# An FFT mixing and balanced mixture-of-experts kernel: pieces of the last fold and of the weight turns, lists of eight in the rounds, and another pace for the gathers

## The chip, the cores and the metric

The kernel runs on one core of a Trainium2 chip. Its time is the device time of one execution in microseconds (us). The kernel before took 535.88 us, the median of three runs (535.51 to 536.1). All five engines of the core take part: TensorE (PE in the profile), VectorE (DVE), ScalarE (ACT), GpSimd (POOL) and SyncE (SP). Each engine works through its own list of instructions in order and waits for the others by semaphores. "PEclk" in the profile is the share of TensorE's full clock that was granted.

## The reference

The input x has 8 batches of 2496 rows by 256 columns. The first step takes the real part of a two-dimensional Fourier transform of each batch; its 19968 rows are the tokens of the second step.

```python
X = np.fft.fft(x, axis=1); X = np.fft.fft(X, axis=2); x = X.real
logits = x @ w_gate                       # 19968 tokens, 8 experts
order = np.argsort(-logits.flatten())     # best pair of token and expert first
for idx in order:
    tok, e = idx // E, idx % E
    if assigned[tok] >= 0 or counts[e] >= cap: continue    # cap = 2496
    assigned[tok] = e; counts[e] += 1
for e in range(E):
    out[assigned == e] = np.maximum(x[assigned == e] @ w1[e], 0) @ w2[e]
```

Every expert takes exactly 2496 tokens: an expert that is full turns tokens away, and they fall to their next choice. The hidden width is 1024.

## The kernel before

**Front (0 to about 90 us).** For each batch `b`, SP and POOL load the rows and their mirror image (`a_t`, `b_t`), and DVE adds them (the fold, L343 and L344). Folded, a batch is 10 blocks of 128 rows, in 5 groups of 2 (index `i` in the change). `zb` is then summed from the fold (L361, L362). `turn_x` transposes the folded batch on PE in three chunks (tp, L285) and ACT copies them out (zt, L287). `gate_x` multiplies the three chunks by the gate's table (yps, L295), into three column groups of one output tile, and ACT copies the result (yt, L298 and L299). `place_y` transposes and stores it as a high and a low part (ytp L305, yhl L308 and L309). In the loop, `gate_x` of batch b - 1 stands between the second and the third chunk of batch b. Behind the loop follow the logits (lps, L452 to L455) and their copy `lg` (L469), laid out as 128 partitions by 8 experts by 160 columns.

**Middle (about 100 to 172 us).** `unit()` issues one of 40 transform units: PE products (fftps, L1038), sums and differences on DVE (stage, L1021 and L1022), and copies on ACT and POOL. It alternates with `first_chain()`, which makes the first choice of experts on DVE: `choose` (each token's best expert), `count` (how many tokens exceed the cap), `lowest` (the lowest logits in each partition, transposed into `lt` on PE, L627), `search` (each turn tries 16 thresholds for each expert and counts, L646, then combines on PE, L657), and `first_strips`, which fixes the tokens that are certain (lev_ps L839, rps L854). The functions are generators. Each `yield` gives an estimated DVE cost, and `yield SYNC` marks the places where PE must wait for DVE. `unit()` keeps two clocks from these estimates and decides how many units come ahead of each step. Four of the units also issue `turn_w`, which folds the transform's last table into an expert's first weight (wps, L1058, four times two matmuls, evicted on ACT). `sort_call` (sps, L1098) gathers the tokens that are certain into strips, which serve as tiles of 384 rows of one expert.

**Experts (172 us to the end).** `experts()` walks over 40 strip tiles of 384 rows and 16 late tiles. Tile j is treated in three parts; in each, `up` does part of the first product of tile j (hps, L1234) and `down` one block of 128 rows of the second product of tile j - 1 (ops, L1257). The result goes to an output tile of a ring, and POOL writes its rows by an indirect DMA, the scatter (L1261). A full tile has three scatters. `take` evicts each product on ACT or DVE, whichever has less estimated work (L995 on ACT, L999 and L1001 on DVE).

Beside the strip tiles run the three rounds of `settle_rest()`, which settle the uncertain tokens: `choose`, `lowest`, `search`, `settle` (the new threshold, transposed on PE at L690), then the token lists of the late tiles (`slots`, `inverse` with inv_ps at L766). `pace(j)` issues these steps by credit: each part of a tile adds 1.9 (at most 3.0), each step takes its estimate off, and a `SYNC` ends the part. When the steps are through, at tile `placed[0]`, the ring grows from 8 output tiles to 18, and `feed` may issue the late tiles' gathers, three indirect DMAs on POOL for each (L1210). They go onto POOL's list between the scatters, and `turn` transposes what they bring (L1222) shortly before the late tile is used. The condition that paces gather m is

```python
j >= min(max(placed[0] + 1 + m * (51 - placed[0]) // 15, 0 if m < 8 else 32), 38 + m)
```

Of the kernel before, what the change touches and what calls it, by code (L numbers as in the profile page):

```python
# [8 lines left out]
FT = mybir.dt.float32  # L9
BF = mybir.dt.bfloat16  # L10
# [25 lines left out]
K_PEN = 1.0e20  # L36
# [17 lines left out]
KC = 56  # L54
# [14 lines left out]
def kernel(  # L69
# [220 lines left out]
    def gate_x(b, zts):  # L290
        yps = psl.tile([P, 4, P], FT, tag="y", bufs=2, name="yps")
        for blk in range(2):
            for c, zt in enumerate(zts):
                nn = 4 if c < 2 else 2
                nc.tensor.matmul(yps[32 * c:32 * c + 32, 0:nn, :], lhsT=g_sb[:, blk, :], rhs=zt[:, blk, 0:nn, :],  # L295
                                 start=(blk == 0), stop=(blk == 1))
# [44 lines left out]
    for b in range(B):  # L341
        a_t, b_t = ab.pop(b)
        nc.vector.tensor_tensor(a_t[:, :, :, 1:D], a_t[:, :, :, 1:D], b_t[:, :, ::-1, D - 1:0:-1], op=AL.add)  # L343
        nc.vector.tensor_tensor(a_t[:, :, :, 0], a_t[:, :, :, 0], b_t[:, :, ::-1, 0], op=AL.add)  # L344
# [17 lines left out]
        nc.vector.tensor_tensor(zb[:, :, P + 1:D], pv[:, :, 1:P], pv[:, :, D - 1:P:-1], op=AL.subtract)  # L362
        zts[b] = [turn_x(b, pv, 0), turn_x(b, pv, 1)]
        if b > 0:
            gate_x(b - 1, zts.pop(b - 1))
# [154 lines left out]
    off = dd.rearrange("p e c -> p (e c)").bitcast(BF)[:, 0:E * GC].rearrange("p (e c) -> p e c", c=GC)  # L520
    ohb = asg.tile([P, E, GC], BF, name="ohb")
    mx = asg.tile([P, GC], FT, name="mx")
    tree = asg.tile([P, 4, GC], FT, name="tree")
    lists = asg.tile([P, E, 8], FT, name="lists")
    lists_x = asg.tile([P, 8, P], FT, name="lists_x")
    cjunk = asg.tile([P, P], BF, name="cjunk")
# [52 lines left out]
    def choose(first):  # L579
        if first:  # L580
            src = lg
        else:
            nc.vector.tensor_tensor(off, lg, tsel[:, :, None].to_broadcast([P, E, GC]), op=AL.is_lt)
            yield 1.5
            nc.vector.scalar_tensor_tensor(wa, in0=off, scalar=-K_PEN, in1=lg, op0=AL.mult, op1=AL.add)
            yield 1.5
            src = wa
# [5 lines left out]
        yield 1.2  # L593
        nc.vector.tensor_tensor(off, src, mx[:, None, :].to_broadcast([P, E, GC]), op=AL.is_lt)
        yield 1.5
        chosen["src"] = src

    def count():
        cps = misc()
        for c in range(0, GC, NG):  # L600
            nc.tensor.matmul(cps[:, 0:P], lhsT=onesb, rhs=off[:, :, c:c + NG], start=(c == 0), stop=(c + NG == GC))
        less = small("less")
        nc.vector.scalar_tensor_tensor(cjunk, in0=cps[:, 0:P], scalar=-1.0, in1=bdiag, op0=AL.mult, op1=AL.mult,
                                       accum_out=less)
        nc.vector.tensor_scalar(exc, in0=less, scalar1=float(P * GC - CAP), scalar2=None, op0=AL.add)
# [3 lines left out]
    def lowest(deep_):  # L609
        nc.vector.scalar_tensor_tensor(wa, in0=off, scalar=-K_LOW, in1=chosen["src"], op0=AL.mult, op1=AL.subtract)  # L610
        yield 1.5
        step = 32 // deep_
        for e in range(E):
            nc.vector.max(lists[:, e, :], wa[:, e, :])
            if e % 4 == 3:
                yield 1.3
            if (e + 1) % step == 0:
                es = slice(e + 1 - step, e + 1)
                nc.vector.tensor_copy(lists_x.rearrange("p j (e g) -> p j e g", g=NG)[:, 0:deep_, es, :],
                                      lists[:, es, 0:deep_].rearrange("p e j -> p j e")[:, :, :, None].to_broadcast(  # L620
                                          [P, deep_, step, NG]))
                yield 0.5
        yield SYNC
        count()
        lt = psr[0].tile([P, deep_, P], FT, tag="lt", bufs=1, name="lt")
        for j in range(deep_):
# [6 lines left out]
        nc.vector.tensor_reduce(lo0, lt[:, deep_ - 1, :], axis=AXX, op=AL.max)  # L633
        wid = small("wid")
        nc.vector.tensor_tensor(wid, hi0, lo0, op=AL.subtract)
        yield 1.2
        found["low"], found["wid"], found["lo0"], found["n"] = lo0, wid, lo0, deep_ * P

    def search(turns):
        junk = wa.rearrange("p e c -> p (e c)")[:, 0:found["n"]]  # L640
        for _ in range(turns):
# [12 lines left out]
            yield 0.9 + found["n"] / 850.0  # L654
# [8 lines left out]
    def settle():  # L663
        low, wid, lo0, ltf = found["low"], found["wid"], found["lo0"], found["ltf"]
        junk = wa.rearrange("p e c -> p (e c)")[:, 0:found["n"]]
# [4 lines left out]
        yield 0.4 + found["n"] / 850.0  # L670
        nc.vector.scalar_tensor_tensor(junk, in0=junk, scalar=-1.0e34, in1=ltf, op0=AL.mult, op1=AL.add)
        yield 0.1 + found["n"] / 900.0
        best = small("best", 8)
        nc.vector.max(best, junk)
        yield 0.1 + found["n"] / 900.0
# [11 lines left out]
        yield 1.6  # L687
# [3 lines left out]
        nc.vector.tensor_scalar(tsel, in0=bps[:, 0:P:NG], scalar1=-1.0, scalar2=None, op0=AL.mult)  # L691
        yield 0.2

    def round_steps(deep_, turns):
        yield from choose(False)
        yield from lowest(deep_)
        yield from search(turns)
# [41 lines left out]
    def inverse(hi1, lo1, pay, w, ncol):  # L739
        ramp8 = ramps[8]  # L740
        inv_ps = psr[0].tile([P, 512], FT, tag="lt", bufs=1, name="inv_ps")
        for c0 in range(0, ncol, 8):
# [6 lines left out]
            o_eq = moe.tile([P, 8, EW + 2], BF, tag="pt", bufs=2, name="o_eq")  # L749
            if w <= P:  # L750
                o_hi = o_eq.rearrange("p a b -> p (a b)")[:, 0:8 * w].rearrange("p (h c) -> p h c", c=8)
                nc.vector.tensor_tensor(o_hi, ramp8[:, 0:w, :], hi1[:, None, cs].to_broadcast([P, w, 8]),
                                        op=AL.is_equal)
                nc.vector.tensor_tensor(o_hi, o_hi, pay[:, None, cs].to_broadcast([P, w, 8]), op=AL.mult)
                o_hi = o_hi.rearrange("p h c -> p c h")
            else:
                o_hi = o_eq[:, :, 0:w]
# [646 lines left out]
```

## Time and profile before

| | us |
|---|---|
| median of three runs | 535.88 |
| the profiled execution | 536.1 |
| its span, first to last instruction | 534.3 |
| PE busy in the span | 471.8 (88%) |
| DVE busy | 372.7 (70%) |
| ACT busy | 337.9 (63%) |
| POOL busy | 313.9 (59%) |

The profile is one execution, taken by the hardware profiler. Its span is 1.8 us shorter than the time of that execution; the rest lies outside the first and last instruction. A line of a group view names the source line, engine, operation, tiles and shapes, then the count, the busy time and the mean duration in ns, then the idle time of the engine just before these instructions and what ended it. A line of a timeline gives start and duration in us, and in square brackets the idle time before it. A table by stretch gives, for each stretch of the span, its length and the busy time and number of instructions of each engine, then the granted clock, the share of the DMA engines and GB/s. In a list of waits, the columns are the total time, how many waits, and the longest.

### The profile page before, as it was taken

To read this page: it belongs to the slowest core of one execution; us is meant where nothing else is said; L and a number is where in the kernel's file an instruction comes from. 1 tells how busy PE (TensorE), PEld (TensorE's weight loads), DVE (VectorE), ACT (ScalarE), POOL (GpSimd) and SP (SyncE) were. 2 spreads that over 40 slices of the span, in tenths; PEclk is the share of its full clock that TensorE was granted. 3 is DMA by queue.
4 is the path that set the end of the run, shared out by engine and by line. 5 is a ranking of instruction groups with operands and counts; after the bars stand their busy time and mean duration, and the time that the engine had idled before them with its cause. 6 is when DMAs were issued, how large, how long until landed. Compare 5 with 4: busy or idle time off the path is not lost.

```text
span 534.3 us, 11232 instructions
## 1 busy us (share of the span) xinstructions
PE 471.8 (88%) x4039; PEld 357.7 (67%) x4039; DVE 372.7 (70%) x952; ACT 337.9 (63%) x762; POOL 313.9 (59%) x362
## 2 busy tenths in 40 slices
PE   0567659899789899999899999999999999999983
PEld 0544436776568566777667877777777777777753
DVE  7799994687978969889978757566654555555431
ACT  7879983156368778788767776556555555555531
POOL 7888815253122555555524336777677777777774
PEclk9968898999989999999989999999999999999988
DMA  8999929078578697523322323342222222222221
GB/s 259 317 281 319 310 89 159 2 240 291 140 217 261 161 225 163 137 95 103 99 76 100 99 88 102 113 130 85 82 83 78 79 87 84 79 69 78 77 77 53
DMA packets 35168, 74.62 MB, mean 140 GB/s; under 512 B 6115, under 2 KB 14349, under 8 KB 35104
## 3 DMA queue, kind: packets, MB, share of 16 engines
q0 software_dynamic: 23296, 42.10, 30.2%
q1 hardware_dynamic: 11808, 31.73, 17.7%
q8 instruction: 33, 0.54, 0.4%
q14 instruction: 31, 0.25, 0.2%
HBM read 51.26 MB, written 32.24 MB: 156 GB/s over the span
## 4 chain that ended last, share of the span: by engine, by line
PE 70%; DVE 13%; ACT 9%; issue 4%; DMA 3%; POOL 1%; POOLq 0%; DVEq 0%; ACTq 0%
PE hps L1234 24%; PE ops L1257 24%; PE sps L1098 5%; PE fftps L1038 5%; PE wps L1058 2%; PE tp L285 2%; ACT zt L287 2%; DMA xa<-in_x_dram 2%; PE yps L295 1%; ACT tf L254 1%; POOL out_dram L1261 1%; DVE xa L343 1%; PE inv_ps L766 1%; DVE stage L1022 1%; PE tp L1222 1%
## 5 line engine op out<-in xcount | busy, mean ns | idle before, releaser
L995 ACT ACTIVATE hb<-hps 128x384 bf16<-128x384 f32 (+1 forms) x326 | 146.2, 493 | 50.5 <-PE hps L1234 47.4
L1257 PE MATMUL ops<-w2t,hb 128*128 128x256 bf16 (+1 forms) x1344 | 175.3, 274 | 0.0
L1257 PEld LDWEIGHTS <-hb 128*128 128x128 bf16 (+1 forms) x1344 | 133.3, 100 | 32.6 <-issue 0.5
L1261 POOL DMA_INDIRECT out_dram<-zball,rid x85 | 89.3, 1051 | 82.7 <-ACT zball L995 63.8
L1234 PE MATMUL hps<-xs,zball 128*128 128x384 bf16 x640 | 127.3, 327 | 0.0
L1234 PEld LDWEIGHTS <-zball 128*128 128x128 bf16 x896 | 86.1, 98 | 43.4 <-issue 2.9
L999 DVE TENSOR_SCALAR hb<-hps 128x384 bf16<-128x384 f32 (+1 forms) x122 | 66.3, 549 | 47.2 <-PE hps L1234 39.2
L129 POOL DMA_INDIRECT xb<-in_x_dram,mir_i x40 | 54.3, 1357 | 11.9 <-issue 10.5
L995 ACT ACTIVATE zball<-ops 128x256 f32<-128x256 f32 (+1 forms) x79 | 30.4, 384 | 31.6 <-PE ops L1257 29.0
L1234 PE MATMUL hps<-xt,zball 128*128 128x384 bf16 (+1 forms) x256 | 48.4, 322 | 0.0
L285 PE MATMUL tp<-identf,xa 128*128 128x128 f32 x160 | 27.4, 336 | 20.1 <-issue 9.2
L285 PEld LDWEIGHTS tp<-identf,xa 128*128 128x128 f32 x160 | 23.6, 176 | 27.1 <-issue 10.2
L995 ACT ACTIVATE xs<-sps 128x384 bf16<-128x384 f32 x68 | 30.4, 493 | 16.0 <-PE sps L1098 15.7
L1026 POOL COPY stage<-stage 128x258 bf16<-128x258 bf16 x40 | 17.7, 447 | 36.3 <-DVE stage L1021 33.0
L1098 PE MATMUL sps<-pt,xl 128*128 128x192 bf16 x320 | 33.8, 246 | 0.7 <-DVE pt L1076 0.7
L1076 DVE TENSOR_SCALAR pt<-rampw,spot 128x193 bf16<-128x193 bf16 x160 | 32.5, 298 | 1.6 <-PE inv_ps L766 0.9
L1098 PEld LDWEIGHTS <-xl 128*128 128x128 bf16 x320 | 27.6, 98 | 3.5 <-issue 1.6
L1210 POOL DMA_INDIRECT xg<-t_dram,ids_l x24 | 23.1, 964 | 7.3 <-issue 7.3
L1261 POOL DMA_INDIRECT out_dram<-zball,rows_l x23 | 22.3, 969 | 7.3 <-issue 2.4
L1044 ACT COPY ev<-fftps 128x512 f32<-128x512 f32 x20 | 11.7, 584 | 22.9 <-PE fftps L1038 15.5
L1001 DVE COPY zball<-ops 128x256 f32<-128x256 f32 (+1 forms) x29 | 12.3, 424 | 19.4 <-PE ops L1257 19.4
L1024 ACT ACTIVATE stage<-stage 128x254 bf16<-128x254 bf16 x40 | 15.6, 414 | 13.3 <-DVE stage L1021 11.6
(356 smaller groups left out, 781.1 us busy)
## 6 DMA issues: line engine op xcount, KB each, us to landing
t_dram<-stage SPq DMA_DIRECT2D x20, 512.0 KB
xl<-t_dram SPq DMA_DIRECT2D x20, 512.0 KB
xa<-in_x_dram SPq DMA_DIRECT2D x8, 1024.0 KB
w1raw<-in_moe_w_dram POOLq DMA_DIRECT2D x8, 512.0 KB, 5.3
w2t<-in_moe_w_dram POOLq DMA_DIRECT2D x8, 512.0 KB, 6.3
xa<-in_x_dram SPq DMA_DIRECT2D x8, 224.0 KB
out_dram<-zball,rid POOLq DMA_INDIRECT x85, 2.5
xb<-in_x_dram,mir_i POOLq DMA_INDIRECT x40, 8.0
```

The source lines that it names most:

```text
L129: nc.gpsimd.indirect_dma_start(out=bv[0:n, i, :], out_offset=None, in_=x_pairs, in_offset=bass.IndirectOffsetOnAxis(ap=mir_i[0:n, b * NK + ...
L285: nc.tensor.transpose(tp[:, blk, u, :], pv[:, 4 * c + u, blk * P:(blk + 1) * P], identf)
L995: nc.scalar.activation(dst, src, ACT.Relu if relu else ACT.Copy)
L999: nc.vector.tensor_scalar(dst, in0=src, scalar1=0.0, scalar2=None, op0=AL.max)
L1026: nc.gpsimd.tensor_copy(st[:, :, 1 + q, 0:P + 1], st[:, :, 3 * q, 0:P + 1])
L1038: nc.tensor.matmul(fps[:, :, d0:d1], lhsT=tab[:nv, i, ks], rhs=zball[:nv, b0:b0 + NB, 2 * i + r, d0:d1], start=(i == 0), stop=(i == NK - 1))
L1076: nc.vector.tensor_scalar(marks[n][:, f, 0:EW + 1], in0=rampw[:, 0:EW + 1], scalar1=spot[:, c:c + 1], scalar2=None, op0=AL.is_equal)
L1098: nc.tensor.matmul(sps[:, j2 * EW:(j2 + 1) * EW], lhsT=xl[:, 2 * g + cc, j2 * P:(j2 + 1) * P], rhs=pt[:, 2 * g + cc, 0:EW], start=(cc == 0 ...
L1210: nc.gpsimd.indirect_dma_start(out=xg[0:nr, q, :], out_offset=None, in_=t_dram, in_offset=bass.IndirectOffsetOnAxis(ap=d["ids"](q, nr), ax ...
L1234: nc.tensor.matmul(hps[:, 0:n], lhsT=w1t[d["e"]][:, j2, fc * P:(fc + 1) * P], rhs=d["x"](j2), start=(j2 == 0), stop=(j2 == 1))
L1257: nc.tensor.matmul(ops[0:nr, 0:D], lhsT=d["hid"][:, fc, b0:b0 + nr], rhs=w2t[d["e"]][:, fc, :], start=(fc == 0), stop=(fc == F // P - 1))
L1261: put = nc.gpsimd.indirect_dma_start(out=out, out_offset=bass.IndirectOffsetOnAxis(ap=d["rows"](b0 // P)[0:nr], axis=0), in_=ot[0:nr, :], ...
```

## The change

It has four parts.

- In the front, the last batch's fold (b = 7) is made in three pieces (groups 0 and 1, 2 and 3, 4), and the gate product of batch 6 is moved ahead of the last batch's transposes. `gate_x` goes through the chunks in the outer loop and through the two halves in the inner one.
- In the middle, the weights of experts 0 to 3 are turned in 16 pieces of two matmuls and one eviction, one after each of the units 15 to 22, 26 to 29 and 33 to 36, instead of whole turns after the units 18, 22, 28 and 34.
- In the rounds, the lists hold 8 values per partition and expert throughout (4 before, in the rounds), so the search and settle passes are 1024 wide instead of 512; there are three search turns in a round instead of two, and one more in the first settling. The choice works expert by expert and sums as it goes (`cnt`), and `count` takes one fp32 product of these sums instead of ten bf16 products over the whole table. The late lists have 64 values per partition instead of 56, hence 8 blocks in `inverse` instead of 7, and their one-hot tiles are written in another layout. Several estimates are changed.
- The gathers are paced at one for every 1.5 tiles from the tile behind `placed[0]`.

```diff
-        for blk in range(2):
-            for c, zt in enumerate(zts):
+        for c, zt in enumerate(zts):
+            for blk in range(2):
...
-        nc.vector.tensor_tensor(a_t[:, :, :, 1:D], a_t[:, :, :, 1:D], b_t[:, :, ::-1, D - 1:0:-1], op=AL.add)
-        nc.vector.tensor_tensor(a_t[:, :, :, 0], a_t[:, :, :, 0], b_t[:, :, ::-1, 0], op=AL.add)
+        for i0, i1 in ((0, 2), (2, 4), (4, NK)) if b == B - 1 else ((0, NK),):
+            nc.vector.tensor_tensor(a_t[:, i0:i1, :, 1:D], a_t[:, i0:i1, :, 1:D], b_t[:, i0:i1, ::-1, D - 1:0:-1],
+                                    op=AL.add)
+            nc.vector.tensor_tensor(a_t[:, i0:i1, :, 0], a_t[:, i0:i1, :, 0], b_t[:, i0:i1, ::-1, 0], op=AL.add)
...
+        if b == B - 1:
+            gate_x(b - 1, zts.pop(b - 1))
         zts[b] = [turn_x(b, pv, 0), turn_x(b, pv, 1)]
-        if b > 0:
+        if 0 < b < B - 1:
             gate_x(b - 1, zts.pop(b - 1))
...
-            nc.vector.tensor_tensor(off, lg, tsel[:, :, None].to_broadcast([P, E, GC]), op=AL.is_lt)
-            nc.vector.scalar_tensor_tensor(wa, in0=off, scalar=-K_PEN, in1=lg, op0=AL.mult, op1=AL.add)
+            for e in range(E):
+                nc.vector.tensor_scalar(wa[:, e, :], in0=lg[:, e, :], scalar1=tsel[:, e:e + 1], scalar2=0.0,
+                                        op0=AL.add, op1=AL.min)
+            nc.vector.scalar_tensor_tensor(wa, in0=wa, scalar=K_PEN, in1=lg, op0=AL.mult, op1=AL.add)
...
-        nc.vector.tensor_tensor(off, src, mx[:, None, :].to_broadcast([P, E, GC]), op=AL.is_lt)
+        for e in range(E):
+            nc.vector.scalar_tensor_tensor(dd[:, e, :], in0=src[:, e, :], scalar=0.0, in1=mx, op0=AL.add,
+                                           op1=AL.is_lt, accum_out=cnt[:, e:e + 1])
+        nc.vector.tensor_copy(cnt_x.rearrange("p (e g) -> p e g", g=NG), cnt[:, :, None].to_broadcast([P, E, NG]))
...
-        for c in range(0, GC, NG):
-            nc.tensor.matmul(cps[:, 0:P], lhsT=onesb, rhs=off[:, :, c:c + NG], start=(c == 0), stop=(c + NG == GC))
+        nc.tensor.matmul(cps[:, 0:1], lhsT=cnt_x, rhs=onesf, start=True, stop=True)
...
+    def finish_round():
+        yield from search(1)
+        yield from settle()
+
-    def round_steps(deep_, turns):
+    def round_steps():
         yield from choose(False)
-        yield from lowest(deep_)
-        yield from search(turns)
+        yield from lowest()
+        yield from search(3)
         yield from settle()
...
-        yield from settle()
+        yield from finish_round()
         for _ in range(NROUND - 1):
-            yield from round_steps(4, 2)
+            yield from round_steps()
...
+    TURNS = (*range(15, 23), *range(26, 30), *range(33, 37))
+    pieces = (None for e in range(4) for _ in turn_pieces(e, "A"))
...
-            if clock["n"] in (18, 22, 28, 34):
-                turn_w((18, 22, 28, 34).index(clock["n"]), "A")
-                clock["PE"] += 2.0
+            if clock["n"] in TURNS:
+                next(pieces)
+                clock["PE"] += 0.45
...
-        while m < len(late) and placed and j >= min(max(placed[0] + 1 + m * (51 - placed[0]) // 15, 0 if m < 8 else 32), 38 + m):
+        while m < len(late) and placed and j >= min(max(placed[0] + 1 + (3 * m) // 2, 0 if m < 8 else 32), 38 + m):
```

## The prediction

> **What bounds the kernel now.** I read the page first: TensorE (PE) is busy for 88% of the span and the chain that ended last gives it 70%. That hides a second limit, so next came the table of busy time by stretch, POOL's timeline, PE's waits and DVE's groups by shape.
>
> The stretches (length, then busy time and count for PE, PE's weight loads, DVE, ACT, POOL, then PE's granted clock):
>
> ```profile
> 77.80:80.90 3.10, 0.82 (x9) 0.84 (x9) 3.10 (x4) 1.52 (x5) 0.61 (x1) 1.00 0.00 0
> 80.90:84.30 3.40, 3.40 (x19) 2.28 (x19) 2.10 (x2) 2.03 (x2) 3.40 (x8) 0.50 0.73 107
> 149.10:152.60 3.50, 3.50 (x19) 2.45 (x18) 1.75 (x5) 1.84 (x5) 1.56 (x3) 0.51 0.77 173
> 178.00:181.40 3.40, 1.35 (x12) 1.10 (x13) 2.81 (x10) 1.04 (x3) 2.65 (x3) 1.00 0.01 1
> 268.60:272.00 3.40, 3.40 (x16) 2.09 (x15) 1.62 (x4) 2.46 (x5) 0.00 (x0) 0.50 0.44 147
> 328.10:529.10 201.00, 195.82 (x1642) 151.34 (x1639) 106.27 (x240) 106.78 (x229) 151.11 (x155) 0.99 0.27 88
> ```
>
> In the last row POOL looks 75% busy, but its timeline shows indirect DMAs at a fixed step, about 0.97 us of work and 0.30 us of issue. From the first gather at 328.16 to the end of the last scatter:
>
> ```profile
> 328.16 1.01 POOL L1210 DMA_INDIRECT xg<-t_dram,ids_l  x1 [0.31 <-issue]
> 329.48 0.97 POOL L1210 DMA_INDIRECT xg<-t_dram,ids_l  x1 [0.30 <-issue]
> ...
> 351.18 0.97 POOL L1261 DMA_INDIRECT out_dram<-zball,rid  x1 [0.57 <-DVE zball L1001]
> 352.46 0.98 POOL L1210 DMA_INDIRECT xg<-t_dram,ids_l  x1 [0.30 <-issue]
> ...
> 528.13 0.93 POOL L1261 DMA_INDIRECT out_dram<-zball,rows_l  x1 [0.30 <-issue]
> ```
>
> That is 155 DMAs (48 gathers, 107 scatters) in 200.9 us. Summing the idle stretches beyond 0.30 us gives 2.89 us, so a step costs (200.9 - 2.89) / 155 = 1.2775 us and POOL has been full since 328. PE runs at the same pace because its output tiles and late inputs pass through POOL. The end is therefore the time at which POOL meets the first gather, plus the number of DMAs from there times 1.2775, plus 5.2 us to the end of the span and 1.8 us outside it (the profiled run: 536.1 us, span 534.3).
>
> PE's waits ahead of that, by line (total, times, longest):
>
> ```profile
> PE wps L1058 <- ACT zball L995: 2.6, 2, 2.1
> PE misc L690 <- DVE trun L686: 2.1, 1, 2.1
> PE lev_ps L839 <- DVE s_lev L834: 1.3, 1, 1.3
> PE rps L854 <- DVE ohb L844: 1.0, 1, 1.0
> ...
> PE misc L601 <- DVE dd L594: 2.7, 1, 2.7
> PE tp L1222 <- DMA xs<-t_dram,ids_l: 2.3, 2, 1.4
> ```
>
> The last line is the last gather coming late (0.82 and 1.45 us near 511). The others say where PE lost time before POOL became the limit.
>
> **The gathers: +6.1 us.** The change paces gathers at 1.5 strip tiles each, from the tile after the lists are placed. The longer rounds place them later: in the changed kernel's instruction order the first gather stands behind 73 scatters (three for each of tiles 0 to 23, and one), where it stood behind 61. Behind it stand 48 gathers and 95 scatters, 143 DMAs in place of 155. The slot after the 73rd scatter is, in the trace of before, the one at 352.46. So POOL would end at 352.46 + 143 x 1.2775 = 535.14 instead of 529.06: +6.1 us, less s, the time by which PE reaches that place earlier. The same by parts: 24.3 later, 15.3 less to issue, 2.9 no longer idle. The step is certain to 0.01 us (gathers 0.96 + 0.30, scatters 0.98 + 0.30), 1.4 us over 143.
>
> After the first gather, a strip tile has 3 scatters and two thirds of 3 gathers, 5 x 1.2775 = 6.39 us of POOL against 5.44 us of PE (two tiles took 10.87). Up to tile 47, POOL falls 22 x 0.95 = 21 us behind, then regains 1.6 us a tile. The last gather has 30 scatters behind it (before: 14), so it is issued at about 535 - 30 x 1.2775 = 496.8 us and is no longer late: PE gains the 2.27 us, and the half clock of 1.7 us behind them, and the end gains nothing, since POOL still has those 30 to issue. PE ends some 13 to 20 us before POOL. Some 14 of the 18 output tiles then wait; were the ring to fill, PE would stop and POOL, which sets the end, would not: priced at 0, and at 0 too if that cover is gone.
>
> Now s, part by part.
>
> **Last fold in pieces, gate first: s +3.1 (1.0 to 3.6).** In 77.80 to 80.90 PE did 0.82 us of work while DVE folded the last batch (L343, 2.81 us); the next 3.4 us ran at a clock of 0.50, a loss of 1.7. The gate moved ahead (eight matmuls, 2.49 us at half clock, about 1.7) fits the hole; the first transposes then need two fifths of the fold. So 1.7 + 1.7, less 0.34 for four more DVE instructions. Low end: the half clock stays and the gate's ACT copies delay the zt copies (1.77) queued behind them. The gate's loop order (column groups) is priced at 0, at worst 0.45 a batch in this stage. ACT was nearly full there, so that could take 3 more.
>
> **Turns in pieces: s +0.35 (-2.2 to +2.6).** Sixteen pieces of two matmuls replace four turns of eight: equal PE work, equal ACT evictions. Gone are waits of 2.1 and 0.46 at wps (the page's 2.6), and the half clock behind (1.7). But the choice runs eight instructions with sums where one ran (below), so it reaches PE's order later: laying the new order on old durations gives new gaps of 2.0 in all, 2.0 before lev_ps (was 1.3) and 1.9 before rps (was 1.5). 4.27 - 2.0 - 0.7 - 0.4 = 1.2. The rows show idle time of 2.11 followed by half clock, and 2.09 not followed by it (the 178.00 row: 1.00), so two gaps of 2 us in a row may halve it again: half of a window, 0.85, is taken off.
>
> [...] The rows above show drops behind 2.1 and 2.7 us. [...]
>
> **First settling: s +1.7 (1.0 to 2.1).** PE waited 2.1 us at L690 for settle. An added search turn moves that transposition behind four or five more PE groups, leaving about 0.35.
>
> **Rounds: s -0.8 (-5 to +2).** DVE's durations, from 128x1024 and 128x512 lists and by expert:
>
> ```profile
> L646 DVE TENSOR_SCALAR_CACHE_REDUCE wa<-lt,s_cand 128x1024 f32<-128x1024 f32 x2 | 2.6, 1285 | 0.1
> ...
> L646 DVE TENSOR_SCALAR_CACHE_REDUCE wa<-lt,s_cand 128x512 f32<-128x512 f32 x6 | 4.5, 751 | 0.2
> L594 DVE TENSOR_TENSOR dd<-wa,mx 128x1280 bf16<-128x1280 f32 x4 | 6.0, 1488 | 0.1
> ```
>
> Choosing: eight instructions of 128x160 at 0.24 to 0.33 for one of 1.49, eight with sums at 0.33 + 0.08 for one of 1.49, a copy, less 0.29 for the old count: +2.5, four times. Lists: +0.42. Search, three turns of 1.285 for two of 0.751 and 1.03 of small ones: +3.4. Settle (0.75, 0.69, 0.70 become 1.28, 1.22, 1.23): +1.6. Three rounds of these 5.4; one more turn, 2.3; inverse, eight blocks for seven with wider-striding one-hots, 4. Sum 9.9 + 16.3 + 2.3 + 4 = 32 us of DVE. It was idle for 28 us of 180 to 328, and the stretch grows by 24: hidden there at about the old share of 81%. Uncovered it would cost PE what exceeds this, the rival below. What reaches PE: the 2.7 at L601 and the half clock behind (1.7) go; a search turn (about 1.8 us with its small instructions) must fit a third of a tile (1.81), and over the twelve places this leaves 0.1 to 0.85 us at seven, 3.35 in all: +1.1. PE's own work: counts -1.8, 12 transposes +1.8, 4 search products +0.7, 8 inverse products +0.9, and evictions pushed to a busier DVE 0.3: -1.9.
>
> **Sum.** s = 3.1 + 0.35 + 1.7 - 0.8 = 4.35; +6.1 - 4.35 = +1.75 on the profiled 536.1. The median of the three times, 535.88, is 0.2 lower: 537.6.
>
> **The rivals.** (1) Not slower: the early savings outweigh the later gathers. This decides at s = 6.1; with no new half clock (+0.85) and new search gaps of 1 us instead of 3.35, s is 7.6 and the time 534.4. For: idle in PE's order is what the change fills. Against: DVE is longer on every chain that PE waits for. (2) PE bounds, POOL doesn't: then the late gather's 2.27 and 1.7 go as well, 535.88 - 4.35 - 4 = 527.5. Against: POOL's fixed step since 328. (3) DVE becomes the bound of the rounds: evictions queue behind passes of 1.3 us, each of twelve turns costs PE 0.7 more, with one half clock in the rounds, 1.7: s loses 10, 547.7; half of it, 542.6. For: DVE and ACT were 81% and 76% busy. (4) The front doesn't do what it says (transposes wait for the whole fold, half clock stays): s loses 2, 539.6.
>
> **How the numbers follow.** Forecast with (4): 0.58, of which two in three lie above +1.07 us (0.2%, about what a measurement of this kernel can tell from no change); (1) 0.20, with (2) 0.04; (3) 0.18. Slower 0.38 + 0.17 = 0.55; faster 0.04 from (2), 0.16 from (1), 0.04 from the forecast's low end; same 0.21. The range leaves out (2) and the worst of (3): 533 to 542; the forecast's own is 535 to 540.5.
>
> **What would show it.** Right: POOL without idle time from the first gather (near 348) to the end, 143 DMAs, PE's last matmul 13 us or more before the last scatter, no wait at L1222's successor. Front: full clock at 78 to 85, logits (L452 before) starting near 87. Wrong: idle stretches in POOL behind the first gather, a first gather later than 351 or sooner than 345, or half clock in the rounds.

## The result and the profile after

The changed kernel took 543.83 us (median of four runs, 543.31 to 545.83) beside 535.99 us for the kernel before: a ratio of 1.0154, 95% interval 1.0128 to 1.0181, or 7.8 us slower. I had forecast slower, 537.6 us, with a range up to 542; the measured time lies 1.8 us above it. The profiled execution took 543.89 us with a span of 542.1 (before: 536.1 and 534.3). Some executions of a kernel fall into a slower state and are left out of every ratio here, so a ratio need not be the quotient of the two times beside it.

The frame of the forecast held. POOL's timeline in the changed kernel, start and duration, with the idle time before each DMA in brackets:

```profile
355.04 1.01 POOL L1218 DMA_INDIRECT xg<-t_dram,ids_l  x1 [0.30 <-issue]
...
536.76 0.93 POOL L1269 DMA_INDIRECT out_dram<-zball,rows_l  x1 [0.30 <-DMA out_dram<-zball,rows_l]
```

From the first gather (behind 73 scatters) to the end of the last scatter stand 143 DMAs without one stretch of idle time above the 0.30 us of issue: (537.69 - 355.04) / 143 = 1.2773 us a step. PE's last product ended at 524.5, 13 us earlier, and no late tile waited for its gather. What failed is the place of the first gather: 355.04, where I had 348.1 (352.46 less 4.35). That is later than 351, which I had named as a sign of being wrong. The table by stretch shows the same places as before (length, then busy time and count for PE, PE's weight loads, DVE, ACT and POOL, then the granted clock):

```profile
77.80:80.90 3.10, 3.10 (x22) 1.51 (x20) 3.10 (x8) 2.30 (x6) 0.00 (x0) 1.00 0.00 0
80.90:84.30 3.40, 3.17 (x28) 2.71 (x28) 3.06 (x4) 2.99 (x6) 3.06 (x4) 1.00 0.46 49
149.10:152.60 3.50, 3.50 (x34) 2.95 (x33) 3.31 (x12) 2.80 (x7) 1.77 (x4) 1.00 0.59 140
...
323.20:326.40 3.20, 0.46 (x8) 0.60 (x9) 2.88 (x7) 0.39 (x1) 0.97 (x1) 0.88 0.43 158
326.40:329.80 3.40, 3.40 (x24) 2.31 (x23) 2.74 (x6) 1.37 (x3) 0.00 (x0) 0.61 0.00 0
355.00:537.70 182.70, 169.53 (x1418) 131.69 (x1415) 91.25 (x198) 93.52 (x201) 139.38 (x143) 0.97 0.26 82
```

The hole at 78 is filled and the half clock behind it is gone, as is the one at 149. New is 323 to 330: PE idle, then at 0.61 of its clock, in the rounds, which was another of those signs. PE's waits in the changed kernel, first the longest of the front, then one of the middle stage, then those behind 185 us (total, times, longest):

```profile
PE lps_cO L456 <- issue: 1.5, 1, 1.5
...
PE lev_ps L840 <- DVE stage L1023: 3.0, 1, 3.0
...
PE inv_ps L767 <- DVE o_eq L761: 2.7, 1, 2.7
PE misc L662 <- DVE s_part L656: 2.1, 3, 1.1
PE sps L1104 <- DVE pt L1082: 1.3, 2, 0.7
PE misc L695 <- DVE trun L691: 1.0, 2, 0.8
PE lt L632 <- DVE lists_x L624: 0.8, 1, 0.8
PE pps L722 <- DVE wa L727: 0.5, 1, 0.5
PE misc L720 <- DVE dd L723: 0.4, 1, 0.4
```

The two lines that my sum does not know are the first (a wait in the logits) and the one at inv_ps (the head of the inverse). How far PE was ahead of the kernel before (s) at five places of the two traces:

| place | before | after | s |
|---|---|---|---|
| first logits product | 90.41 | 88.03 | +2.4 |
| first transform product | 100.53 | 99.83 | +0.7 |
| first down product | 176.92 | 176.24 | +0.7 |
| down product of the third tile | 193.42 | 190.42 | +3.0 |
| first down product of tile 24 | 349.41 | 352.03 | -2.6 |

Each column is one execution, and one stretch of half clock more or less (3.41 us at 0.50) moves a figure by 1.7 us.

### The profile page after: what moved, and what is told of

Read it like the earlier page. It is cut to its first block, busy times and chain, and to the rows that moved or that the text cites. A ratio compares the mean times of both kernels' runs of the same rounds, so it can differ in the third digit from the quotient of the medians.

```text
span 542.1 us, 11340 instructions
## 1 busy us (share of the span) xinstructions
PE 469.0 (87%) x4023; PEld 355.7 (66%) x4023; DVE 387.2 (71%) x1067; ACT 345.2 (64%) x786; POOL 312.4 (58%) x362
## 5 line engine op out<-in xcount | busy, mean ns | idle before, releaser
L1269 POOL DMA_INDIRECT out_dram<-zball,rid x95 | 97.2, 1023 | 100.3 <-ACT zball L996 90.5
L1000 DVE TENSOR_SCALAR hb<-hps 128x384 bf16<-128x384 f32 (+1 forms) x117 | 63.5, 548 | 42.4 <-PE hps L1242 34.0
L996 ACT ACTIVATE zball<-ops 128x256 f32<-128x256 f32 (+1 forms) x97 | 37.3, 384 | 37.0 <-PE ops L1265 32.8
L285 PE MATMUL tp<-identf,xa 128*128 128x128 f32 x160 | 29.0, 350 | 17.0 <-ACT hi_cE L258 7.4
L285 PEld LDWEIGHTS tp<-identf,xa 128*128 128x128 f32 x160 | 24.9, 184 | 24.4 <-ACT hi_cE L258 7.8
L996 ACT ACTIVATE xs<-sps 128x384 bf16<-128x384 f32 x73 | 32.3, 491 | 9.9 <-PE sps L1104 8.6
L1025 ACT ACTIVATE stage<-stage 128x254 bf16<-128x254 bf16 x40 | 15.8, 414 | 13.0 <-DVE stage L1022 10.8
L1002 DVE COPY zball<-ops 128x256 f32<-128x256 f32 (+1 forms) x21 | 8.9, 424 | 19.9 <-PE ops L1265 19.9
```

What stands on the lines that cost most here:

```text
L285: nc.tensor.transpose(tp[:, blk, u, :], pv[:, 4 * c + u, blk * P:(blk + 1) * P], identf)
L996: nc.scalar.activation(dst, src, ACT.Relu if relu else ACT.Copy)
L1000: nc.vector.tensor_scalar(dst, in0=src, scalar1=0.0, scalar2=None, op0=AL.max)
L1025: nc.scalar.activation(st[:, :, 1 + q, P + 1:D], st[:, :, 3 * q, P + 1:D], ACT.Copy, bias=0.0, scale=-1.0)
L1269: put = nc.gpsimd.indirect_dma_start(out=out, out_offset=bass.IndirectOffsetOnAxis(ap=d["rows"](b0 // P)[0:nr], axis=0), in_=ot[0:nr, :], ...
```

## The experiments

I call P the theory of the prediction: from the first gather on POOL's list sets the end. Q is its rival: PE's own order sets it and POOL follows.

| run | kernel | time | before, same chip | ratio, 95% interval | first gather | DMAs from there | end of last scatter |
|---|---|---|---|---|---|---|---|
| e1_pace | before + new pace | 532.91 | 535.9 | 0.9962, 0.9933 to 0.9992 | 326.37 | 155 | 524.29 |
| e2_front | before + front | 532.8 | 535.9 | 0.9946, 0.9922 to 0.997 | 326.38 | 155 | 527.19 |
| e3_turns | before + turns in pieces | 536.19 | 535.9 | 1.001, 0.9982 to 1.0037 | 328.96 | 155 | 529.72 |
| e4_rounds | before + rounds | 546.96 | 535.9 | 1.0214, 1.018 to 1.0248 | 356.96 | 143 | 540.70 |
| e5_after_cut | after, 18 scatters left out | 544.37 | 535.85 | 1.0167, 1.0135 to 1.02 | 355.08 | 125 | 527.40 |
| e6_after_keys | after, one estimate larger | 542.7 | 535.85 | 1.0129, 1.0105 to 1.0154 | 357.02 | 140 | 536.44 |
| e7_front_late | front, w2 loads later | 536.61 | 535.85 | 1.0026, 1.0007 to 1.0046 | 328.14 | 155 | 528.90 |
| e8_front_pace_late | the same + new pace | 534.14 | 535.85 | 0.9986, 0.9964 to 1.0008 | 328.40 | 155 | 526.46 |

Ten more runs fell on chips where the kernel before itself took 586 to 595 us; they stand at the end. The "same chip" column is the median of the kernel before there, whose executions went from 532.3 to 537.9 us on the chip of e1 to e4 and from 533.4 to 537.7 on that of e5 to e8.

### The four parts alone

**The new pace.** Edit:

```diff
- j >= min(max(placed[0] + 1 + m * (51 - placed[0]) // 15, 0 if m < 8 else 32), 38 + m)
+ j >= min(max(placed[0] + 1 + (3 * m) // 2, 0 if m < 8 else 32), 38 + m)
```

> The kernel before with only the new pace of the gathers (one for 1.5 tiles). Theory P (POOL is full from the first gather on, and the end is that gather plus the DMAs from there at 1.277 us): the first gather stays behind 61 scatters at 328.2, 155 DMAs follow as before, and only the 2.9 us of idle stretches go: the last scatter ends at 526.2 instead of 529.06 and the time is 533.0 (532.5 to 533.6). Rival Q (PE's own order sets the end, POOL follows): the late gather's waits of 0.82 and 1.45 us and the half clock of 1.7 us behind them go, so 4 us: 532.0. Under P, PE ends some 4 us before the last scatter; under Q the two keep their distance of 2.9 us.

532.91 us, near P's 533.0; Q's 532.0 lies 0.9 us away, and the interval is 1.6 us wide to each side, so the time alone does not decide between them. POOL's timeline of this run, the first gather and the last scatter:

```profile
326.37 1.01 POOL L1210 DMA_INDIRECT xg<-t_dram,ids_l  x1 [0.30 <-issue]
...
523.36 0.93 POOL L1261 DMA_INDIRECT out_dram<-zball,rows_l  x1 [0.30 <-issue]
```

(524.29 - 326.37) / 155 = 1.277 us, without idle stretches; PE ended at 520.1, 4 us ahead, which is P's picture and not Q's 2.9. The pace by itself is a gain: it takes out POOL's idle time. Of the 4.8 us by which this run's last scatter is earlier, 2.9 are that; 1.8 come from an earlier first gather, because this execution had no half clock behind the wait at L601 (1.00 from 268.6 to 272.0, where before had 0.50). That is chance of the execution (see the part on the clock below).

**The front.** Edit: the hunks of the fold, of `gate_x` and of its place, from the diff above.

> The kernel before with only the front (last fold in three pieces, gate of the batch ahead first, the gate's loop order). In the changed kernel the first transform unit started 0.7 us earlier, though the logits started 2.4 us earlier: 1.5 us were lost in a wait inside the logits that the profile calls issue. Theory P carries whatever PE gains here to the first gather and to the end: 535.2 if that wait is there again, 533.6 if it was chance or belongs to another part of the change. My prediction's figure for this part, 3.1 us, would give 532.8. Rival: a gain in the front is eaten by the next wait in the middle, 535.9.

532.8 us: 3.1 us less (1.6 to 4.2 by the interval). In the profile the logits start 3.15 us earlier than in before (87.26), at full clock. But the wait is there again:

```profile
PE lps_cO L456 <- issue: 1.5, 1, 1.5
```

so the first transform product is only 1.46 us ahead (99.07), and the first gather 1.8. With the wait there I had expected 535.2, and the median is 2.4 us under that. That it equals my prediction's 3.1 us is not borne out by the trace: the profiled execution took 534.34 us, 1.8 less than the profiled one of before. Why the others gained more is not shown.

**The turns in pieces.** Edit: `turn_pieces`, `TURNS` and the call in `unit()`, from the diff above.

> The kernel before with only the weight turns of experts 0 to 3 in pieces. With the old choice and the old lists in place, the waits of 2.1 and 0.46 us at the turns and the half clock behind them (1.7 us) should go, and the chain of the first choice is not longer: 532.5 if nothing takes their place. In the changed kernel the middle stage as a whole gained nothing (0.71 us ahead at its start, 0.68 at the first down product), but there the longer choice ran in it: if the pieces themselves are at fault, 535.9. P and Q do not differ here.

536.19 us, no difference: the pieces themselves gain nothing. The waits at wps are gone as in the forecast, and this is what takes their place, with the old choice and the old lists:

```profile
PE lev_ps L839 <- DVE stage L1022: 3.1, 1, 3.1
```

That wait was 1.3 us before, for the level itself. Now PE comes sooner to the place where it needs DVE's chain, and waits there; the clock falls to 0.60 behind it (132.6 to 136.0).

**The rounds.** Edit: all the hunks of `choose`, `count`, `lowest`, `search`, `settle`, `finish_round`, `round_steps`, `inverse` and the constants.

> The kernel before with only the rounds of the changed kernel (lists of eight, three turns, sums by expert, 64 values). Theory P: the first gather stands behind 73 scatters and PE reaches it about 0.7 us later than in the changed kernel, at 355.7; 143 DMAs take it to 538.4, and the time is 544.6 to 545.4. PE waits for late gathers near the end, since the old pace puts the last gather 14 scatters before the end (about 519), but that costs nothing beyond. Rival Q: PE's waits for late gathers come on top of its own later order: 544.5 plus those 10 us, 554. A third theory, that the change loses its time by the parts working together and not by the rounds, would give 538 or less.

546.96 us, 11 us more: the whole loss of the change, and more, is in the rounds. The first gather and the last scatter of the run:

```profile
356.96 1.01 POOL L1207 DMA_INDIRECT xg<-t_dram,ids_l  x1 [0.30 <-issue]
...
539.77 0.93 POOL L1258 DMA_INDIRECT out_dram<-zball,rows_l  x1 [0.30 <-issue]
```

P had 355.7 and 538.4, and 544.6 to 545.4 for the time, so the time lies 1.6 us above it. In the profiled execution the logits started 1.5 us later than in before (91.89), and 1.16 us of idle time came near the end. Q's 554 is refuted. PE waited 6 us for late gathers (L1219), and nearly all of it cost nothing, as POOL was full. The 1.16 us are what it did cost: there (532.75 to 535.94) POOL waits for the evictions of PE's late products, and the last scatter ends 2.8 us behind PE's last product (537.87).

The parts' differences are -3.0, -3.1, +0.3 and +11.1, together +5.3, each known to 1.3 to 1.8 us; the whole has +7.8. With the new rounds POOL has next to no idle time left, so the pace has nothing to take out: without its 3 us the sum is 8.3.

### Is it POOL that sets the end?

Edit to the changed kernel: `down` returns ahead of the scatter for the strip tiles 32 to 37.

```diff
+        if d.get("silent"):
+            return
         put = nc.gpsimd.indirect_dma_start(
...
+    for d in tiles[32:38]:
+        d["silent"] = True
```

> The changed kernel without the scatters of the strip tiles 32 to 37: 18 of the 143 DMAs behind the first gather are left out (those rows of the output are not written); PE, ACT and DVE do all their work. Theory P (POOL's list sets the end): POOL would be through at 355.0 + 125 x 1.277 = 514.7, before PE's last product at 524.5, so PE becomes the limit, the last scatter ends some 3 us behind it at 527.5, and the time is 533.7, 10 us less. Theory Q (PE's own order sets the end): nothing changes, 543.8.

The last scatter ended at 527.40, which is P's 527.5, and PE's last product again at 524.6. The time did not fall: 544.37. Three stretches of that run, same columns as above:

```profile
355.00:421.00 66.00, 66.00 (x553) 50.51 (x552) 36.99 (x90) 36.99 (x84) 50.37 (x52) 1.00 0.26 82
421.00:527.40 106.40, 103.58 (x868) 81.20 (x865) 54.27 (x108) 56.58 (x117) 71.11 (x74) 1.00 0.21 68
527.40:542.60 15.20, 0.00 (x0) 0.00 (x0) 0.00 (x0) 0.00 (x0) 0.00 (x1) 0.50 0.02 5
```

For the last 15 us no engine has work. In the trace POOL's sequencer is in its closing DRAIN for 9.14 us (532.62 to 541.76), where before and after have 1.71, and the semaphore instruction ahead of it took 2.42 instead of 0.59. Together that is 9.3 of the 10.8 us by which the end of the span lies further behind the last scatter than in the changed kernel. By time alone this run looks like Q's; by its scatters it is P's: taking DMAs off POOL's list moved the last scatter by 10.3 us, to 3 us behind PE. With 18 unread gathers put in early, so that the program has its old number of DMAs (e9, f4 and g2 below), the DRAIN took 1.84 us in all three. Only these two numbers of DMAs were measured (9.14 us at 198, 1.71 to 1.84 at 216), and why the times differ is open. That the time falls as well when POOL has fewer DMAs and the DRAIN is short was not shown on a chip where POOL sets the end.

### The wait at the inverse

PE's and DVE's timelines of the changed kernel at 322 to 326 us:

```profile
322.16 1.03 PE L1265 MATMUL ops<-w2t,hb 128*128 128x256 bf16 x8
325.94 0.64 PE L767 MATMUL inv_ps<-o_eq,oh 128*128 128x48 bf16 x8 [2.74 <-DVE o_eq L761]
```

```profile
324.13 0.69 DVE L755 TENSOR_TENSOR oh<-ramp,l_lo 128x1024 bf16<-128x1024 bf16 x1 [0.21 <-DMA xl<-t_dram]
324.74 0.55 DVE L759 TENSOR_TENSOR o_eq<-rampw,l_hi 128x384 bf16<-128x384 bf16 x1
325.33 0.56 DVE L761 TENSOR_TENSOR o_eq<-o_eq,l_pay 128x384 bf16<-128x384 bf16 x1
```

DVE is still building the first one-hot tiles when PE asks for them. The estimate in the code for one step of the late lists had been lowered from 0.75 to 0.6, while a step takes 0.33 + 0.09 + 0.31 us. Edit to the changed kernel:

```diff
-            yield 0.6
+            yield 1.0
```

> The changed kernel with the estimate of one step of the late lists (the largest eight values of a partition and their removal) at 1.0 instead of 0.6, so that PE is given more tile work before it meets the inverse. If the wait of 2.74 us ahead of the first inverse product and the half clock behind it (1.65 us) come from an estimate that is too small: both go, the first gather stands behind 76 scatters instead of 73 (a tile later, 5.4 us, less those 4.4: 356.1), 140 DMAs follow, the last scatter ends at 534.9 and the time is 541.0. If DVE is simply too slow there, the wait stays and the tile is added: 355.0 + 5.4 + 178.8 = 539.2, 545.4.

The waits at inv_ps fell to 0.25 and 0.74 us, and the clock stayed full:

```profile
325.00:328.40 3.40, 2.93 (x27) 2.18 (x25) 3.33 (x13) 2.12 (x6) 1.41 (x2) 1.00 0.22 77
328.40:331.80 3.40, 2.88 (x31) 2.45 (x31) 2.79 (x5) 1.84 (x5) 1.44 (x1) 1.00 0.13 43
```

The first gather came at 357.02 (expected 356.1, without the two waits that are left), the last scatter ended at 536.44 instead of 537.69, at 1.282 us a step. The time is 542.7 (expected 541.0), 1.1 us less than the changed kernel's, and the intervals of the two ratios overlap. So the wait was one of estimates, and removing it gives back little, since the cover is a tile of PE work that puts the first gather later.

### The wait inside the logits

It came only with the front, at 92.28 alone and at 93.05 in the changed kernel, always 5 us into the logits, and lasted 1.5 us. In both traces a load of 16 KB of instructions ran just ahead of it (91.38 to 92.34; 92.10 to 93.06), among the packets of the weights (w1raw and w2t, in transfer until about 93 to 94). In before this load runs from 93.02 to 93.98, as the weights end, and the same products run after 95. Edit to the front alone:

```diff
             load_w1(1)
-            load_w2(wts[0])
-            load_w2(wts[0])
...
+    load_w2(wts[0])
+    load_w2(wts[0])
     for c in first_chain():
```

> The kernel with the front alone, and the loads of w2 for experts 0 and 1 (1 MB of the 2 MB that POOL issues in the last batch) moved behind the logits, ahead of the first choice. Theory: the wait of 1.52 us inside the logits, which came at 93.05 in the changed kernel and at 92.28 with the front alone and ends when the weight loads do, is PE's own code arriving behind those loads. Then it goes, the transform starts at 97.6 instead of 99.07, and the time is 1.5 us under the front alone: 531.3 to 532.8. Rival: the wait belongs to something else of the front and stays, 532.8 to 534.3 as before.

The wait is gone: from the first logits product (87.92) to the first transform product (98.05) it took 10.1 us, as in before, instead of 11.8. The 16 KB load now runs from 89.45 to 90.39, behind the last weights (88.4). That agrees with PE's code arriving behind the weights, but does not show it: where the wait came, it began just as the load ended (92.28 and 92.34; 93.05 and 93.06), and other contents of these DMAs were not tried. And the time is 536.61, where 531.3 to 532.8 was expected. PE's and DVE's waits in that run:

```profile
PE fftps L1040 <- DVE stage L1024: 4.8, 4, 2.8
...
DVE stage L1023 <- DMA t_dram<-stage: 4.8, 2, 3.8
```

The moved megabyte now meets the writes of the transform (t_dram), DVE waits 3.8 us for its stage buffer, and the 1.5 us are lost again and more: 2.5 us ahead of before at the first transform product, PE is 1.9 us behind it at the first down product (178.83).

> The kernel before with the front, with the loads of w2 moved as in the run above, and with the new pace of the gathers; the rounds and the weight turns are those of before. Theory P: the gains add, as each moves the first gather or takes idle time out of POOL behind it: first gather at 328.2 - 1.8 - 1.5 = 324.9, 155 DMAs at 1.277 to 522.8, time 529.0 to 529.8. If the wait in the logits stays, 530.5 to 531.3. Rival: with POOL served, something on PE bounds: the time stays at that of the new pace alone, 532.9.

534.14 us, 4 to 5 us above what I expected, for the same reason (3.5 us ahead at the first transform product, 0.4 behind at the first down product): first gather at 328.40 instead of 324.9, then 155 DMAs in (526.46 - 328.40) / 155 = 1.278 us each. The rival's "PE bounds" is not shown: PE ended 4.3 us ahead of POOL. Beside e7, the pace took 2.5 us off, as POOL's 2.8 us of idle time went; alone it took 3.0.

### Ten runs on chips where PE waits for something unnamed

On three more chips the kernel before took 595.43, 586.01 and 594.0 us (labels with e, f and g). Edits: the front and the pace on the kernel before (e10, f1, g1); the changed kernel with credit 2.3 for 1.9 in `pace` (e11, f2); with `search(2)` for `search(3)` and without the added turn (e12, f3); and the cut of e5 with 18 unread gathers early (e9, f4, g2).

> The kernel before with the front and the new pace of the gathers, all loads where they were. Theory P: first gather at 326.4 as with the front alone, behind 61 scatters, no idle stretches behind it (2.9 us in the kernel before), 155 DMAs at 1.277 us to 524.3; time 530.4 to 531.3, that is 0.990 to 0.991 of before. Rival: PE bounds once POOL is served, 532.9 as with the pace alone.

> The front and the new pace on the kernel before, once more. On the chip of the last four runs the kernel before took 595 us and PE waited some 50 us behind 330 for nothing that the profile names, so POOL had idle time there and the question stayed open. Where the kernel before takes about 536, theory P: first gather at 326.4, 155 DMAs without idle time to 524.3, time 530.4 to 531.3. Rival: PE bounds once POOL is served, 532.9.

> The front and the new pace of the gathers on the kernel before, a third time, for a chip where the kernel before takes about 536. Theory P: first gather at 326.4, 155 DMAs without idle time to 524.3, time 530.4 to 531.3 (0.990 to 0.991 of before). Rival: PE bounds once POOL is served, 532.9 (0.994). Where the kernel before takes 586 or more, the two runs so far gave 0.999 and 1.005, and the same is expected.

591.16, 588.07 and 591.38 us, first gathers at 328.1, 323.4 and 328.0. Ratios 0.9991 (0.9943 to 1.0038), 1.0053 (1.0015 to 1.0092) and 1.0006 (0.9968 to 1.0043): no gain there. PE's weight loads in the last of them, behind 341 us, waited for

```profile
PEld L1238 <- issue: 36.5, 40, 3.8
PEld L1102 <- issue: 4.6, 3, 3.2
...
```

nothing that the profile names, 46.7 us in all (0.4 us in e1_pace between 330 and 525). POOL, with steps of 1.28 us as elsewhere, had 57 us of idle time behind the first gather: on these chips PE sets the end, and serving POOL better gained nothing (0.9991 to 1.0053). Whether the waits are for PE's code was not settled. That front and pace add where the kernel before takes 536 us was therefore not shown.

> The changed kernel with a credit of 2.3 instead of 1.9 for each part of a tile, so that the rounds' steps come faster and the first gather stands behind 61 scatters, as before, instead of 73. Theory P: four tiles less of PE (21.8 us) ahead of the first gather, 12 DMAs more behind it (15.3), and w us of new waits on PE, since DVE has the same work in a shorter stretch: first gather at 333.2 + w, last scatter at 531.1 + w, time 537.4 + w. With w between 1 and 6 that is 538.5 to 543.4, under the changed kernel. If the rounds' DVE work is simply too much for four tiles less (32 us more of it, where DVE had 28 us idle), w is over 6.4 and the time is 543.8 or more.

> The changed kernel with a credit of 2.3, once more. On the slower chip its first gather came at 344.1 where it stood behind 61 scatters and the changed kernel's rows of before had 333.2, so w, the new waits on PE, is about 9 to 11 us (waits of 2.85, 4.49 and 2.24 us at single places of the rounds). Theory P, where the kernel before takes about 536: last scatter at 342 to 344 + 155 x 1.277 = 540 to 542, time 546 to 548, above the changed kernel. If the slower chip made those waits, 538.5 to 543.4 as first expected.

605.69 and 601.97 us, ratios 1.0239 (1.0156 to 1.0321) and 1.032 (1.0262 to 1.0379). What can be read from these runs is how PE waits for DVE in the rounds, in f2_after_credit from 182 to 341 us:

```profile
PE misc L695 <- DVE trun L691: 8.2, 3, 4.5
PE misc L662 <- DVE s_part L656: 3.1, 6, 1.1
PE misc L915 <- DVE s_flagb L913: 2.2, 1, 2.2
...
```

With the three small ones it is 16 us, where the changed kernel has 8.8. The first gather came at 344.1 and 341.5, behind 61 scatters, so w was 10.9 and 8.3, above the 6.4 from which this credit no longer pays. Of the 21.8 us of tiles that no longer stand ahead of the first gather, PE spends 8 to 11 waiting for DVE, and the 12 DMAs more behind it (15.3 us) outweigh the rest. That sum uses first gathers of slower chips; at that place the front and the pace came 3.0 us earlier to 1.7 later there than the 326.4 that was expected.

> The changed kernel with two search turns in each round and none added to the first settling, as before, all else as changed (lists of eight, 1024 wide). The first gather stands behind 67 scatters, 149 DMAs follow. Theory P: two tiles less (10.9 us) ahead, 6 DMAs more (7.7), and about 2 us of PE's waits at the dropped turns gone: 5.2 us less, 538.6. If waits turn up elsewhere in their place, 540.6; if PE's order and not POOL's list set the end, only the waits count, 541.8.

> The changed kernel with two search turns and none added, once more: 67 scatters ahead of the first gather, 149 DMAs behind it. On the slower chip the first gather came at 343.0, some 12 us earlier than the changed kernel's 355.0. Theory P, where the kernel before takes about 536: 341 to 343 + 149 x 1.277 = 531.5 to 533.5, time 537.6 to 539.8. If PE's order and not POOL's list set the end, only the dropped turns' waits count: 541.8.

600.91 and 595.27 us, ratios 1.0149 (1.0039 to 1.0259) and 1.0168 (1.011 to 1.0225), first gather at 343.0 and 340.5 behind 67 scatters, with about 5 us of waits for DVE in the rounds. By P's count those starts and 149 DMAs would give a last scatter near 533.3 and 530.8, 4 to 7 us ahead of the changed kernel's 537.7, as an estimate. The absolute times expected can't be compared, and the changed kernel itself was not run there, so the share of the search turns in its loss stays open.

> The changed kernel again without the scatters of the strip tiles 32 to 37 (those rows of the output are not written), but with 18 more gathers of strip rows, which nobody reads, behind the scatters of the tiles 9 to 14, where POOL has idle time. The number of indirect DMAs is that of the changed kernel. In the run with the scatters merely left out, the last scatter ended at 527.4 as theory P had it (527.5), but POOL's closing DRAIN took 9.14 us instead of 1.71 and the time did not fall. If that DRAIN goes by the number of DMAs in the program, it is 1.71 here, the last scatter ends at about 527.5 and the time is 533.5 to 534.5. If leaving the scatters out late is what lengthens the DRAIN, the time is 544 again. Theory Q (PE sets the end) has 543.8 in any case.

> The changed kernel without the scatters of the strip tiles 32 to 37 and with 18 unread gathers early, once more (those rows of the output are not written). On the slower chip the closing DRAIN was 1.84 us, so it goes by the number of DMAs. Where the kernel before takes about 536, theory P: last scatter at 527.5, time 533.5 to 534.5. Theory Q (PE sets the end): 543.8.

> The changed kernel without the scatters of the strip tiles 32 to 37 and with 18 unread gathers early (those rows of the output are not written), for a chip where the kernel before takes about 536. Theory P: last scatter at 527.5, closing DRAIN 1.7 to 1.9, time 533.5 to 534.5. Theory Q (PE sets the end): 543.8. Where the kernel before takes 586 or more: 1.03 of it or more, as in the two runs so far.

608.72, 607.02 and 608.76 us, ratios 1.0296 (1.0145 to 1.0447), 1.0386 (1.0319 to 1.0453) and 1.0306 (1.0216 to 1.0397). On these chips PE sets the end (in e9 its last product ended 3 us ahead of the last scatter), so they tell about the DRAIN and not about P and Q.

## Why the prediction was wrong

**The limit and the gathers' term: right.** Predicted was "the time at which POOL meets the first gather, plus the number of DMAs from there times 1.2775". Seven of the eight runs at 536 us and the two kernels follow it, with steps of 1.274 to 1.282 us once idle stretches are taken off (none to 2.9 us of them); in e5, with 18 DMAs fewer, POOL has 13 us of idle time, and PE takes over, 3 us ahead. The +6.1 us less s became +6.1 + 2.6 = 8.6 on the last scatter (537.69 - 529.06). The span grew by 7.8 only, as 4.4 us follow the last scatter instead of 5.2. No late gather, PE ending 13 us ahead, no gain from either: as foretold.

**s was mis-sized: 4.35 predicted, -2.6 measured.** Of these 7.0 us the rounds make 4.8 and the front 2.4; 537.6 + 7.0, less the 0.8 behind the last scatter, is the measured 543.8. By its terms:

- *Front*: +3.1 predicted, +2.4 at the logits, +0.7 at the transform. The hole and the half clock went as described (e2: 3.15 at the logits). Missing from the sum was a wait of 1.5 us in logits begun earlier, while the weights are still in transfer; it is the same in both kernels that have the front, and gone in e7, but what it waits for is not shown.
- *Turns*: +0.35 predicted, 0.0 measured in the whole change and no difference alone. The exchange of waits was right in kind; the new one at lev_ps was 3.0 instead of 2.0 (3.1 in e3), and the half clock at 149 is gone in both, though e3 has one behind that wait.
- *First settling*: +1.7 predicted, +2.3 measured.
- *Rounds*: -0.8 predicted, -5.6 measured. This is the step that failed. The waits at the search, the lists and the threshold were 4.0 us (0.76, 0.30, 1.08, 0.81, 0.22 and 0.81) where I had 3.35. What I left out is what follows the rounds: I had priced the 32 us of DVE work as "hidden there at about the old share of 81%", and looked for uncovered places among the search turns only. PE waited 5.0 us for the late lists and the strips beside them (2.74 at the inverse, 0.39 and 0.52 at the slots, 0.70 and 0.62 at sps), and ran 1.5 us longer at the lower clock behind. The waits and clock of before here sum to 5.2 (2.74, 0.74, 1.7), those of after to 10.5; of the 5.6 this leaves about 0.3 us for PE's own added work, where I had 1.9. The loss repeats between the same two places: 5.8 us in e4 and 5.6 in e5, each with 2.8 us at the inverse.

**The clock.** I took off 0.85 us for two gaps of 2 us in the middle, going by the rows. In the changed kernel a gap of 2.99 us at 129.4 was followed by full clock; in e3, one of 3.08 at 129.0 was followed by 0.60; 2.74 at 323.2 was followed by 0.61, and 2.74 at 264.6 in e1 by none, in before by 0.50. In these rows the length of a gap alone does not tell, at 2 to 3 us. The place of the gap differed too. The traces of the two kernels record the changes of the granted clock at whole multiples of 3.4133 us from each other, to 0.001 us (in before at 80.88, 84.29, 149.14, 152.56 and 268.61, in the changed kernel at 325.63 and 329.04). From 90 us to PE's last product, the 3.41 us ahead of a fall to 0.50 held 2.11, 2.42 and 2.01 us of PE's idle time in before and 2.43 in the changed kernel; the other stretches, counted in the same steps, held at most 1.91 (before, 176.45 to 179.86). The 2.74 us in before had 2.42 in one such stretch, and the 2.99 in the changed kernel lie to both sides of 131.07, 1.65 and 1.34. In e1, counted in the same steps from its fall at about 149.7, a point at 265.7 splits the 2.74 into 1.1 and 1.6. But in e4 the clock fell near 512.3 with about 1.6 us of idle time ahead. These are counts from a few executions; what sets the clock was not shown.

**The rivals.** That DVE becomes the bound of the rounds (542.6 to 547.7) was the right direction: 543.8 lies between its two figures. Its mechanism, evictions behind long passes in each search turn, is not what the waits show; they stand at the late lists. That PE bounds (527.5) fell. That the front doesn't do what it says fell in its form (the fold's pieces worked) and came true in size in the changed kernel's trace.

Two versions beat both kernels: the front alone (0.9946) and the new pace alone (0.9962).

## What to carry to other kernels

A queue that is full from some point on turns everything behind that point into a count of its items (here 143 DMAs at 1.277 us); predict the point, and look for every wait ahead of it, those behind the last changed step too. Work that is called hidden must be covered place by place: the estimates that pace it decide whether the other engine arrives early, and raising them costs the tile that covers. Work that starts earlier can meet other transfers: here the front's 3.1 us at the logits were 1.5 at the transform, behind a wait that went when half of the weight loads were moved, and moving them cost more than it gave.

## What I had not expected of the hardware

POOL's closing DRAIN took 9.14 us with 198 indirect DMAs in this part of the program (e5) and 1.71 to 1.84 us with 216 (before, after, e9, f4 and g2). A half clock behind the same wait of 2.74 us appears in one execution and not in another (before: 0.50 from 268.6 to 272.0; e1: 1.00), and e1's first gather came 1.8 us earlier (326.37 instead of 328.16). And the same kernel took 535.9 us on two chips and 586 to 595 us on three others, where in all ten profiles PE's weight loads waited 42 to 58 us behind 341 us for nothing that the profile names.
